# The last term of each block of attention scores, made in two halves of 144 columns

## The chip, the cores and the metric

One Trainium2 chip, one core. The metric is the device time of one execution in microseconds (us). Besides TensorE (PE in the profile; its weight loads are shown apart as PEld) the kernel uses VectorE (DVE), ScalarE (ACT), GpSimd (POOL) and SyncE's DMA queue (SP).

## The reference, cut to what matters

The program is an attention layer with a computed position bias (8 batches, 8 heads, 576 positions, 64 dimensions to a head), followed by a mixture of experts over the 4608 tokens. The change lies in `scores` alone, before the bias is added:

```python
scores = scale * np.matmul(q, k.transpose(0, 1, 3, 2))      # 576 x 576 for each batch and head
scores = scores + bias.transpose(2, 0, 1)[None, :, :, :]
scores = scores - np.max(scores, axis=-1, keepdims=True)
attn = np.exp(scores)
attn = attn / (np.sum(attn, axis=-1, keepdims=True) + 1e-09)
out = np.matmul(attn, v)
# then: softmax gate, the best of 8 experts for each token, relu(x @ w1[e]) @ w2[e], times the gate
```

## The kernel before, in words

The heads are taken two at a time: 32 pairs. The two heads of a pair lie one above the other on the partitions (64 dimensions each), so that a product of head 0 uses rows 0 to 63 of TensorE's array and the same product of head 1 rows 64 to 127. Of each pair the 576 queries make five blocks `c`. Blocks 0 to 3 hold 128 queries of each head; block 4 holds the last 64 queries of both heads, laid out as a block-diagonal tile, and so uses all 128 rows in one product. That makes 32 x 5 = 160 blocks of scores.

`scores` (the matmul is L372) makes one block in the PSUM tiles `sps`, one for each head, two banks each: the 576 keys are two `half`s of HS = 288 columns, one to a bank. `q` and `k` were split before into a high part, rounded to float32r, and the rest (`QK[:, 0]` and `QK[:, 1]`, both float32r, by `high` L338 on ACT and `low` L343 on DVE), and a product is a sum of three terms (`TERMS`): high x high, high x low, low x high, in this order, accumulated in PSUM. A block of two heads has 2 halves x 3 terms x 2 heads = 12 matmuls, head 0 and head 1 in turn; block 4 has 6. Every matmul loads its own weights, 128 query columns (64 or 128 rows).

`biased` (L395, DVE, one for each head) then reads a head's 576 scores from PSUM, adds the bias from `NBm` (block 4: `NBr`) and takes the row's extreme in the same instruction; `exps` (L409, ACT) makes the exponentials and their sums. `etrans` (through `turn`, L324) transposes the exponentials on TensorE, `av` (L488) multiplies them with `v`, in plain float32. There is one pair of `sps` tiles: the next block's first matmul of a head waits for that head's L395.

The order of the work is written out by hand in `ORDER`: five strings to a pair of heads, one step after the other for all engines (S is `scores`, E `exps`, T and t `etrans` and its evacuation, A and a `av`, and so on), pipelined over three pairs. Nothing looks at times; an engine takes its instructions in this order and waits on semaphores.

Behind the attention come the expert tiles: `phase1` (L1336), `phase2` (L1353), then pairs of tiles (L1427, L1439), all in float32r with the same three terms; their weights are read by SP's queue into `NBm`'s space (L1268, L1271) as it comes free.

Of the kernel before, what the change touches and what calls it, by code (L numbers as in the profile page):

```python
# [21 lines left out]
P = 128  # L22
# [6 lines left out]
HS = S // 2  # L29
QW = 512 + P  # L30
# [87 lines left out]
class Attn:  # L118
# [243 lines left out]
    def scores(self, n, c):  # L362

        nc = self.nc
        QK = self.QK[n % 2]
        qs = slice(P * c, P * c + P)
        for half in range(2):
            ks = slice(QW + HS * half, QW + HS * half + HS)
            for i, (a, b) in enumerate(self.TERMS):
                for h in range(2) if c < 4 else (None,):  # L370
                    o = slice(0, P) if h is None else slice(64 * h, 64 * h + 64)
                    nc.tensor.matmul(  # L372
                        self.sps[h or 0][:, half, 0:HS],
                        QK[o, a, qs],
                        QK[o, b, ks],
                        start=i == 0,
                        stop=i == 2,
                        tile_position=(0 if h is None else 64 * h, 0),
                        skip_group_check=True,
                    )  # L380
        self.E[n, c] = self.Eb[:, next(self.e_next)]
        return [self.biased(n, c, h) for h in range(2 if c < 4 else 1)]

# [1457 lines left out]
```

## Time and profile before

| what | value |
|---|---|
| median of 3 runs | 966.83 us (965.53 to 967.01) |
| profiled execution, time and span | 971.9 us, 970.1 us |
| PE busy | 944.8 us (97%), 10430 matmuls |
| PEld busy | 784.2 us (81%), 10430 loads |
| DVE, ACT, POOL busy | 679.0, 632.2, 233.0 us |
| granted TensorE clock, mean | 0.990 |

The span runs from the first to the last instruction of the profiled execution; 1.8 us lie around it. Matmuls are pipelined, and a matmul's row has its whole passage through the array, so neighbours overlap: what a matmul costs in a stream is the distance from one start to the next, not its duration. A pair of matmuls of the two heads starts within some ns of each other, on different rows of the array.

### The profile page before, as it was taken

To read this page: it belongs to the slowest core of one execution; us is meant where nothing else is said; L and a number is where in the kernel's file an instruction comes from. 1 tells how busy PE (TensorE), PEld (TensorE's weight loads), DVE (VectorE), ACT (ScalarE), POOL (GpSimd) and SP (SyncE) were. 2 spreads that over 40 slices of the span, in tenths; PEclk is the share of its full clock that TensorE was granted. 3 is DMA by queue.
4 is the path that set the end of the run, shared out by engine and by line. 5 is a ranking of instruction groups with operands and counts; after the bars stand their busy time and mean duration, and the time that the engine had idled before them with its cause. 6 is when DMAs were issued, how large, how long until landed. Compare 5 with 4: busy or idle time off the path is not lost.

```text
span 970.1 us, 26355 instructions
## 1 busy us (share of the span) xinstructions
PE 944.8 (97%) x10430; PEld 784.2 (81%) x10430; DVE 679.0 (70%) x1528; ACT 632.2 (65%) x1396; POOL 233.0 (24%) x388
## 2 busy tenths in 40 slices
PE   7979999999999999999998999999999999999997
PEld 5448888888888888888887888897577888888885
DVE  7978889899999989999975668855224444353434
ACT  7988889899998999989874555555123423242323
POOL 0002001323142322314633345131104031212111
PEclk9999999999999999999998999999999999999998
DMA  5875312322232233223161112367835320201111
GB/s 148 241 228 150 121 55 91 109 77 90 87 126 84 70 106 102 85 68 125 39 231 52 44 55 85 129 229 267 298 130 175 120 77 11 76 33 55 44 45 47
DMA packets 50586, 106.89 MB, mean 110 GB/s; under 512 B 14033, under 2 KB 16849, under 8 KB 50452
## 3 DMA queue, kind: packets, MB, share of 16 engines
q1 hardware_dynamic: 42676, 84.00, 26.4%
q0 software_dynamic: 7680, 21.10, 6.6%
q8 instruction: 84, 1.38, 0.6%
q14 instruction: 50, 0.41, 0.1%
q10 hardware_dynamic: 96, 0.00, 0.0%
HBM read 118.86 MB, written 22.00 MB: 145 GB/s over the span
## 4 chain that ended last, share of the span: by engine, by line
PE 83%; DMA 6%; issue 5%; SPq 2%; ACT 1%; DVE 1%; POOL 1%; ACTq 0%; DVEq 0%; POOLq 0%
PE sps L372 15%; PE xps L488 9%; PE eps L488 8%; PE p L1427 6%; PE p L1336 5%; PE xps L1439 5%; PE eps L324 5%; PE p L1439 5%; PE xps L324 5%; PE pq L1427 4%; PE bps L201 4%; DMA NBm<-moe_w 4%; PE p L1353 2%; PE xps L1353 2%; PE xps L427 1%
## 5 line engine op out<-in xcount | busy, mean ns | idle before, releaser
L409 ACT ACTIVATE Eb<-Eb,mn 128x576 f32<-128x576 f32 x288 | 223.3, 785 | 10.0 <-DVE mn L395 9.2
L395 DVE CUSTOM_DVE_ANT_0 Eb<-sps,NBm 128x576 f32<-128x576 f32 x256 | 183.3, 753 | 15.7 <-ACT rT L329 5.8
L372 PE MATMUL sps<-QK 64*128 64x288 f32 (+1 forms) x1728 | 175.0, 309 | 3.7 <-DVE mn L395 3.5
L372 PEld LDWEIGHTS sps<-QK 64*128 64x128 f32 (+1 forms) x1728 | 139.2, 188 | 12.3 <-issue 6.6
L1366 POOL DMA_INDIRECT out<-mo,idt x22 | 22.9, 1041 | 254.9 <-ACT mo L1363 243.6
L1429 ACT ACTIVATE hh<-p 128x512 fp32r<-128x512 f32 x28 | 16.8, 599 | 97.6 <-PE p L1427 87.6
L1430 DVE SCALAR_TENSOR_TENSOR hl<-p,hh 128x512 fp32r<-128x512 f32 x28 | 19.4, 691 | 84.0 <-ACT hh L1429 81.9
L488 PE MATMUL xps<-eT,v 128*64 128x160 f32 (+1 forms) x960 | 75.3, 299 | 0.0
L1304 DVE TENSOR_TENSOR w2lo<-NBm,w2hi 128x1024 fp32r<-128x1024 f32 x49 | 60.1, 1226 | 15.8 <-ACT w2hi L1303 15.3
L488 PE MATMUL eps<-eT,v 128*64 128x144 f32 (+1 forms) x992 | 70.7, 283 | 0.0
L418 POOL COPY rem<-Eb 128x128 f32<-128x128 f32 x64 | 18.7, 293 | 206.8 <-ACT Eb L409 172.5
L488 PEld LDWEIGHTS xps<-eT,v 128*64 128x64 f32 x960 | 58.4, 136 | 9.8 <-issue 9.5
L343 DVE TENSOR_TENSOR QK<-qk,QK 128x640 fp32r<-128x640 f32 (+1 forms) x64 | 61.7, 965 | 0.0
L329 ACT COPY eT<-xps 128x512 f32<-128x512 f32 (+1 forms) x127 | 59.3, 501 | 2.3 <-PE eps L324 0.8
L488 PEld LDWEIGHTS eps<-eT,v 128*64 128x64 f32 x992 | 56.6, 138 | 3.1 <-issue 2.8
L1336 PE MATMUL p<-QK,w1hi 128*128 128x256 f32 x384 | 56.4, 291 | 2.0 <-ACT w1hi L1310 2.0
L409 ACT ACTIVATION_READ_ACCUMULATOR Eb<-Eb,mn 128x1 f32 x288 | 57.9, 201 | 0.0
L870 POOL TENSOR_TENSOR xrb<-xrb,rec 128x512 f32<-128x512 f32 (+1 forms) x34 | 35.4, 1042 | 91.1 <-DVE xrb L331 47.9
L1427 PE MATMUL p<-QK,w1hi 128*128 128x512 f32 x224 | 56.0, 392 | 0.4 <-DVE htq L1670 0.4
L1336 PEld LDWEIGHTS p<-QK,w1hi 128*128 128x128 f32 x384 | 51.8, 199 | 2.8 <-ACT w1hi L1310 2.1
L1303 ACT CAST w2hi<-NBm 128x1024 fp32r<-128x1024 f32 x49 | 51.2, 1044 | 3.5 <-DMA NBm<-moe_w 3.5
L1278 POOL DMA_INDIRECT NBr<-xg,idt x40 | 44.0, 1099 | 33.7 <-issue 9.9
(339 smaller groups left out, 2217.7 us busy)
## 6 DMA issues: line engine op xcount, KB each, us to landing
NBm<-moe_w SPq DMA_DIRECT2D x14, 2048.0 KB
NBm<-moe_w SPq DMA_DIRECT2D x28, 1024.0 KB
qk<-qk SPq DMA_DIRECT2D x32, 608.0 KB
NBm<-moe_w SPq DMA_DIRECT2D x32, 512.0 KB
v<-v SPq DMA_DIRECT2D x32, 320.0 KB
xg<-xrb SPq DMA_DIRECT2D x28, 258.0 KB
NBm<-eT SPq DMA_DIRECT2D x10, 288.0 KB
NBm<-eT SPq DMA_DIRECT2D x20, 144.0 KB
```

The source lines that it names most:

```text
L324: self.nc.tensor.transpose(ps[r][0:n, col : col + 64], x[o, :], self.idf[o, o])
L329: self.nc.scalar.copy(out, ps)
L343: self.nc.vector.tensor_tensor(QK[:, 1, sl], self.qk[n][:, sl], QK[:, 0, sl].bitcast(F32), op=ALU.subtract)
L372: nc.tensor.matmul(self.sps[h or 0][:, half, 0:HS], QK[o, a, qs], QK[o, b, ks], start=i == 0, stop=i == 2, tile_position=(0 if h is None e ...
L395: nc.vector.tensor_tensor_reduce(out=e.rearrange("p (t w) -> p t w", t=2), in0=ps, in1=nb.rearrange("p (t w) -> p t w", t=2), scale=self.S ...
L409: self.nc.scalar.activation(e, e, AF.Exp, bias=mn, scale=-1.0, accum_out=sm)
L488: nc.tensor.matmul(ps[o, :], v[:, 4 * D * h + D * k : 4 * D * h + D * k + D] if k < 4 else v[:, 512 + D * h : 512 + D * h + D], eT[:, h, k ...
L1303: self.nc.scalar.copy(h, w)
L1304: self.nc.vector.tensor_tensor(l, w, h.bitcast(F32), op=ALU.subtract)
L1336: nc.tensor.matmul(ps[:, a, :], w[:, c, fs], x[:, c, :], start=i == 0, stop=i == len(ops) - 1)
L1427: nc.tensor.matmul(ps, w[:, c, fs], x[:, c, :], start=j == 0, stop=j == len(ops) - 1, skip_group_check=True)
L1439: nc.tensor.matmul(self.acc[w], h[:, P * w : P * w + P], m[:, f, :], start=f == 0 and j == 0, stop=f == NFC - 1 and j == 2, skip_group_che ...
```

## The change

The third term of the second half of each block (low x high, into columns 288 to 575) is issued as two matmuls for each head, of 144 columns each, into the two parts of the same PSUM columns. The order is: columns 0 to 143 for head 0, then head 1, then columns 144 to 287 for head 0, then head 1. Weights, operands and sums are the same as before. Blocks 0 to 3 have 14 matmuls in place of 12, block 4 has 7 in place of 6; each has its own weight load.

```diff
-            ks = slice(QW + HS * half, QW + HS * half + HS)
+            k0 = QW + HS * half
             for i, (a, b) in enumerate(self.TERMS):
-                for h in range(2) if c < 4 else (None,):
-                    o = slice(0, P) if h is None else slice(64 * h, 64 * h + 64)
-                    nc.tensor.matmul(
-                        self.sps[h or 0][:, half, 0:HS],
-                        QK[o, a, qs],
-                        QK[o, b, ks],
...
+                for ks in halves if (half, i) == (1, 2) else whole:
+                    for h in range(2) if c < 4 else (None,):
+                        o = slice(0, P) if h is None else slice(64 * h, 64 * h + 64)
+                        nc.tensor.matmul(
+                            self.sps[h or 0][:, half, ks],
+                            QK[o, a, qs],
+                            QK[o, b, k0 + ks.start : k0 + ks.stop],
...
```

Here `whole = (slice(0, HS),)`, `mid = HS // 2` and `halves = slice(0, mid), slice(mid, HS)`.

## Rows read from the trace of the kernel before

**Rows 1.** The page: the span, busy time by engine, TensorE's granted clock in 40 slices.
```profile
span 970.1 us, 26355 instructions
...
PE 944.8 (97%) x10430; PEld 784.2 (81%) x10430; DVE 679.0 (70%) x1528; ACT 632.2 (65%) x1396; POOL 233.0 (24%) x388
...
PEclk9999999999999999999998999999999999999998
```

**Rows 2.** The chain of work that ended last, 398 to 414 us: start, length, what.
```profile
400.88 0.98 PE sps L372 x6
401.86 0.65 PE xps L324 x16
402.50 0.50 PE eps L324 x16
403.00 0.91 PE sps L372 x12
403.91 1.51 PE xps L488 x20
405.42 0.34 PE eps L324 x8
405.77 0.87 PE sps L372 x12
406.63 1.38 PE xps L488 x20
408.01 0.64 PE eps L324 x15
```

**Rows 3.** Busy time of the engines in the attention, 110 to 490 us.
```profile
core 0: us, PE busy (x) PEld busy (x) DVE busy (x) ACT busy (x) POOL busy (x), PEclk, DMA share, GB/s
110.00:490.00 380.00, 379.79 (x6386) 330.57 (x6383) 347.02 (x933) 343.27 (x914) 106.92 (x228) 1.00 0.28 91
```

**Rows 4.** All waits of PE, 74 to 500 us: us in total, times, longest.
```profile
PE sps L372 <- DVE mn L395: 0.2, 1, 0.2
```

**Rows 5.** All of L372: durations in ns, shortest, median and longest.
```profile
L372 PEld LDWEIGHTS sps<-QK x1728: 182/185/333, 55.1 to 499.4; 64*128 64x128 f32 x192
L372 PE MATMUL sps<-QK x1728: 286/291/606, 55.1 to 499.6; 64*128 64x288 f32 x192
```

**Rows 6.** Timeline of PE, one block of two heads: start, us, line, tiles, count.
```profile
402.86 1.06 PE L372 MATMUL sps<-QK 64*128 64x288 f32 x12
403.84 1.31 PE L488 MATMUL xps<-eT,v 128*64 128x160 f32 x16
404.98 0.44 PE L488 MATMUL xps<-rT,v 128*64 128x160 f32 x4
```

**Rows 7.** Durations in ns of the same block's loads and matmuls.
```profile
L372 PEld LDWEIGHTS sps<-QK x12: 183/184/187, 402.9 to 403.5; 64*128 64x128 f32 x12
L372 PE MATMUL sps<-QK x12: 288/290/396, 402.9 to 403.6; 64*128 64x288 f32 x12
```

**Rows 8.** Timeline of PE, one block 4 and what follows it.
```profile
400.81 1.05 PE L372 MATMUL sps<-QK 128*128 128x288 f32 x6
401.79 0.59 PE L324 MATMUL xps<-idf,Eb 64*128 64x64 f32 x12
```

**Rows 9.** The chain in the expert tiles: unbroken runs of 256 and of 512 columns.
```profile
619.74 11.53 PE p L1336 x96
...
808.88 5.44 PE pq L1427 x24
```

**Rows 10.** Matmuls by line and shape: count, busy us, mean ns.
```profile
L372 PE MATMUL sps<-QK 64*128 64x288 f32 x1536 | 141.1, 309 | 2.8 <-DVE mn L395 2.7
L1336 PE MATMUL p<-QK,w1hi 128*128 128x256 f32 x384 | 56.4, 291 | 2.0 <-ACT w1hi L1310 2.0
L1427 PE MATMUL p<-QK,w1hi 128*128 128x512 f32 x224 | 56.0, 392 | 0.4 <-DVE htq L1670 0.4
L488 PE MATMUL xps<-eT,v 128*64 128x144 f32 x480 | 36.0, 292 | 0.0
L372 PE MATMUL sps<-QK 128*128 128x288 f32 x192 | 33.9, 312 | 0.8 <-DVE mn L395 0.8
```

**Rows 11.** Weight loads by line and shape, as above.
```profile
L372 PEld LDWEIGHTS sps<-QK 64*128 64x128 f32 x1536 | 112.8, 188 | 5.9 <-DVE mn L395 4.4 <-issue 1.3
L1336 PEld LDWEIGHTS p<-QK,w1hi 128*128 128x128 f32 x384 | 51.8, 199 | 2.8 <-ACT w1hi L1310 2.1
L1427 PEld LDWEIGHTS p<-QK,w1hi 128*128 128x128 f32 x224 | 41.7, 188 | 11.7 <-issue 2.5 <-DVE htq L1670 0.7
L1318 PEld LDWEIGHTS p<-idf,NBr 128*128 128x128 f32 x80 | 9.4, 140 | 1.3
```

**Rows 12.** Timeline of PE: the last early block of scores that waits, and the next.
```profile
70.78 2.48 PE L372 MATMUL sps<-QK 64*128 64x288 f32 x12 [0.99 <-DVE mn L395]
74.50 0.58 PE L372 MATMUL sps<-QK 64*128 64x288 f32 x1
```

**Rows 13.** PE busy and granted clock around that stretch.
```profile
core 0: us, PE busy (x), PEclk, DMA share, GB/s
...
70.00:72.00 2.00, 1.15 (x5) 0.65 1.00 408
72.00:74.00 2.00, 2.00 (x32) 0.50 0.48 103
74.00:76.00 2.00, 2.00 (x28) 0.50 0.31 26
76.00:78.00 2.00, 2.00 (x25) 0.65 0.57 165
```

**Rows 14.** Timeline of SP's queue: the first expert weights.
```profile
483.76 0.42 SPq L1268 DMA_DIRECT2D NBm<-moe_w  x1
501.16 1.07 SPq L1271 DMA_DIRECT2D NBm<-moe_w  x2
```

More of the change, by code (lines that the diff above doesn't have):

```diff
@@ L366, in scores @@
         qs = slice(P * c, P * c + P)
+        whole, mid = (slice(0, HS),), HS // 2
+        halves = slice(0, mid), slice(mid, HS)
         for half in range(2):
-            ks = slice(QW + HS * half, QW + HS * half + HS)
+            k0 = QW + HS * half
             for i, (a, b) in enumerate(self.TERMS):
-                for h in range(2) if c < 4 else (None,):
-                    o = slice(0, P) if h is None else slice(64 * h, 64 * h + 64)
-                    nc.tensor.matmul(
-                        self.sps[h or 0][:, half, 0:HS],
-                        QK[o, a, qs],
-                        QK[o, b, ks],
[L376 to L380, printed above, removed]
+                for ks in halves if (half, i) == (1, 2) else whole:
[5 more added lines that the diff above has]
+                            QK[o, b, k0 + ks.start : k0 + ks.stop],
+                            start=i == 0,
+                            stop=i == 2,
+                            tile_position=(0 if h is None else 64 * h, 0),
+                            skip_group_check=True,
+                        )
         self.E[n, c] = self.Eb[:, next(self.e_next)]
```

## The prediction

> **What bounds the kernel now.** I read the page's engines first, then the chain of waits, then the attention's own engines, and last one block of scores at the scale of single matmuls. The page has PE at 97% of the span [rows 1], but a busy PE means little, since matmul rows overlap. The chain says more: in the attention it runs over PE alone, from one group of matmuls to the next, with no other engine between them [rows 2], and the same holds from 74.5 us to the end of the scores at 499.6 us. In 380 us of that stretch PE has 379.8 us busy, DVE 347.0 and ACT 343.3 [rows 3], and from 74 to 500 us PE waits for another engine just once, for 0.2 us [rows 4]. So TensorE's own issue is the limit, and a nanosecond added to its stream there is a nanosecond added to the time. The one loop beside it, from a block's scores through DVE's two L395 to the next block's scores, begins with the same matmuls, and a later end of them moves it by as much as it moves PE.
>
> **What one block costs.** The 12 matmuls of a block lie in 1.06 us [rows 6], the last takes 0.290, so the last pair starts 0.77 us after the first. The first pair's matmuls take 396 ns and the others 290 [rows 7]: 106 ns more. I read this as a weight load that nothing hides, since these start with their load. The other steps are (770 - 106) / 5 = 133 ns from pair to pair. Block 4 gives (1050 - 290 - 106) / 5 = 131 ns for its single matmuls [rows 8].
>
> What a step consists of, the expert tiles show, which use the same type: 11.53 us / 96 = 120 ns for 256 columns, 5.44 / 24 = 227 ns for 512 [rows 9]. The 107 ns between them are 256 columns at 0.417 ns, one column in a cycle of 2.4 GHz, the level that rows 3 have granted (1.00). So 288 columns stream in 120 ns, 144 in 60, and 11 to 13 ns of a step are fixed.
>
> The weight load is the second clock of a step. Two loads of float32r weights can't follow each other faster than one takes, 106 ns by the first pair. At 288 and 512 columns that is hidden: the load's row is 188 ns in both, and 199 at 256 columns [rows 11], where stream and load are about equal, as if it had begun to be held up. The load's row for plain float32 weights of the same 128 columns is 140 [rows 11], so this type's load is the longer one.
>
> **The change, part by part.** Removed: one step of 288 columns at the end of each block (two matmuls, or one in block 4). Added: two steps of 144. Nothing else moves: no DMA, no DVE or ACT instruction, no wait; L395 waits for the last matmul of its head as before.
>
> - The first half starts where the whole one started; its load runs under the 288 columns ahead of it. Cost nothing; the cover is those 120 ns against a load of 106, and without it this load would add up to 106 ns.
> - The second half needs its own load, although the weights are the same: the kernel issues as many loads as matmuls (10430 of each, [rows 1]), so none is dropped for being the same as the one before. That load can begin when the first half begins to stream, and the first half streams for 60 ns only. So the second half starts not 60 + 13 = 73 ns but 106 + 12 = 118 ns after the first. From both sides: 73 ns if the load is hidden after all, 120 ns by the nearest row, the 256-column step [rows 9]. I take 118, nearest to that row.
> - The second half then streams for 60 ns in place of 120. Behind the block the next group changes the array's tiling (64 or 128 rows, 64 or 128 columns) and starts about 0.21 us after the last scores' start: 403.84 against 402.86 + 0.77 [rows 6], 120 of it the stream and some 90 the change. The 90 stay, and 60 of the 120 go. Block 4's follower has the same distance, 401.79 against 400.81 + 1.05 - 0.29, 0.22 us [rows 8].
>
> Net for each block: 118 + 60 - 120 = +58 ns, from +13 (hidden load) to +60.
>
> Blocks on the path: 160 in all (1536 / 12 = 128 of two heads and 192 / 6 = 32 blocks 4, [rows 10]), the last at 499.6 us [rows 5]. The first seven start before 74.5 us, while PE waits for DVE [rows 12], behind transfers and partly at half clock [rows 13]; of these I count two. 155 x 58 ns = 9.0 us; from 2.0 (13 ns) to 9.3 (60 ns).
>
> What comes later gives none of it back: the experts' first weights are issued at 483.8 and 501.2 us [rows 14], when the bias table's space comes free as the attention ends, so the rest shifts as a whole. DVE and ACT get a longer period for the same work.
>
> One rule of the Trainium skill speaks against the large term: "TensorE: Matmul & The Clock Gate", section "Back-to-back issue gap", gives N / 2.4 + 2.5 ns for a warm matmul on its own, 62.5 ns for 144 columns. By it the estimate is +2.5 ns a block and +0.4 us in all. The rows above have 13 ns where it has 2.5, and the 106 ns of an unhidden load stand against it here; its section "LDWEIGHTS (loading the stationary operand)" in the same page gives columns / 1.2, an estimate of 107 ns for 128, which the trace's 106 agrees with.
>
> **The sum.** The profiled execution took 971.9 us (span 970.1), 5.1 above the runs' median; it gives 971.9 + 9.0 = 980.9. The extra is in the attention's own stream, where the runs don't differ by more than their 1.5 us, so I put it on the median: 966.83 + 9.0 = 975.8.
>
> **The rivals.**
>
> - *The load is hidden (not slower).* Place: between the two halves. If the second load could start under the 288-column matmul ahead, 73 ns or less separate the halves, and the price is 13 ns a block, or 2.5 with a smaller fixed part: 0.4 to 2.0 us, 967.2 to 968.8, within 0.2%. It decides as soon as a load takes under about 73 ns of a step. For it: loads of a pair do run beside the other row half. Against: the 106 ns of a block's first pair, and the 256-column load's longer row. Chance 0.11.
> - *The narrow matmul loses its single pass.* No float32r matmul of this kernel is narrower than 256 columns, so its rate at 144 isn't shown. The plain float32 ones show what such a loss costs: `av` has 10 calls and 20 matmuls [rows 2, 6], each at (404.98 + 0.44 - 403.84 - 0.30 - 0.05) / 9 = 137 ns a pair for 160 columns (0.05 for its first load, half as wide as the scores'); the 144-column group is 0.13 us shorter [rows 2], 13 ns a pair: so two instructions to a product, and two cycles to a column, 123 ns at 144. With both, a block has four steps where one was: 3 x 123 = +369 ns, 57 us, 1024. With two cycles to a column alone, a half costs 120 + 13 and the end streams 120: +133 ns, 20.6 us, 987.4. For it: nothing but that the case is new; against: the rate is the same 0.417 ns from 256 to 512, and 288 lies on the line. Chances 0.14 and 0.10.
> - *Faster.* The half-clock stretch [rows 13] has about 6.8 us at 1.2 GHz and costs some 3.4 us. More matmuls in the blocks just ahead of it could end or move it; with the hidden load that would be 966.83 + 0.4 - 3.4 = 963.8. Against: PE there waits for transfers, which this change doesn't touch. Chance 0.03.
> - *Part of it is absorbed*, in waits of PE that the profile puts down to no one, which come with each change of tiling: +20 to +45 ns a block, 970 to 974. Chance 0.07.
>
> **How the numbers follow.** The forecast has 0.55: 975.8, its own range 974.5 to 977.0 (53 to 63 ns a block on 150 to 160 blocks, and the median's own spread). Beside it stand 0.11 hidden, 0.07 partly absorbed, 0.10 at 987.4, 0.14 at 1024 and 0.03 faster. A range from 967.8 to 988.5 holds the forecast, the absorbed case, the two cycles and most of the hidden case, 0.82; it leaves out the double pass and the faster case. A measurement here can tell about 0.2% (1.9 us) from no change. Slower by more: 0.55 + 0.07 + 0.10 + 0.14 and a little of the hidden case, 0.87; within 0.2%: 0.10; faster: 0.03.
>
> **What would show it.** In the profile after, a block's last weight load starts with the first half and the second half starts some 118 ns behind it; the matmul rows of 144 columns are about 60 ns shorter than the 290 of 288; the next group starts about 0.15 us after the last scores' start; the run from 110 to the attention's end is longer by 58 ns a block and PE waits as little as before. Wrong: halves 73 ns or 133 ns apart, more than 14 (7) matmul records in a block, or 144-column rows of 290 ns and more. If the halves are 118 ns apart and the time grows by much less than 9 us, then my claim that PE's stream alone sets the end is what fails.

## The result and the profile after

| | median, us | lowest to highest |
|---|---|---|
| before | 967.01 (5 runs) | 965.53 to 968.6 |
| after | 975.71 (5 runs) | 973.46 to 976.55 |

The changed kernel takes 1.0088 times as long, with a 95% interval of 1.0071 to 1.0105: 8.7 us more. The forecast was 975.8.

The page after, against [rows 1]:

```profile
span 973.8 us, 26931 instructions
...
PE 949.1 (97%) x10718; PEld 803.7 (83%) x10718; DVE 678.7 (70%) x1528; ACT 631.3 (65%) x1396; POOL 232.0 (24%) x388
...
PEclk9999999999999999999999999999999999999999
```

There are 288 more matmuls and as many more weight loads (10718 of each): 2 x 128 + 32, one for each matmul that became two. The other engines do what they did.

The matmuls and loads of the scores by line and shape (count, busy us, mean ns; L375 after is L372 before), against [rows 10, 11]:

```profile
L375 PE MATMUL sps<-QK 64*128 64x288 f32 x1280 | 122.8, 312 | 2.2 <-DVE mn L398 2.1
L375 PE MATMUL sps<-QK 64*128 64x144 f32 x512 | 47.5, 250 | 0.0
L375 PE MATMUL sps<-QK 128*128 128x144 f32 x64 | 10.9, 252 | 0.0
...
L375 PEld LDWEIGHTS sps<-QK 64*128 64x128 f32 x1792 | 128.6, 186 | 5.0 <-DVE mn L398 3.4 <-issue 1.3
```

The load's row is as long as before (186 against 188 ns), also before a half. The mean of 250 ns for 144 columns hides two kinds, which one block shows. PE's timeline of the block that answers to [rows 6] (start, length in us); the line below the dots is the same view of a window that only the block's last pair reaches into:

```profile
406.18 1.11 PE L375 MATMUL sps<-QK 64*128 64x288 f32 x14
407.22 0.36 PE L491 MATMUL xps<-eT,v 128*64 128x160 f32 x2
...
407.01 0.27 PE L375 MATMUL sps<-QK 64*128 64x144 f32 x2
```

The durations in ns (shortest, median, longest) of this block's matmuls, against [rows 7], and of its last pair alone:

```profile
L375 PE MATMUL sps<-QK x14: 227/291/398, 406.2 to 407.0; 64*128 64x288 f32 x10, 64*128 64x144 f32 x4
...
L375 PE MATMUL sps<-QK x2: 270/270/270, 407.0 to 407.0; 64*128 64x144 f32 x2
```

The first halves take 227 ns, 63 less than the 290 of 288 columns. The second halves take 270: 43 ns longer for the same columns. Their rows begin 66 ns behind the first halves' (starts in the trace, 768 and 834 ns after the block's), so they come to an end 66 + 43 = 109 ns behind them. I read a row that begins on time and lasts 43 ns too long as a matmul that waits inside its row for its weights; since the profile only models the ends of matmul rows, this needs a check by starts, which the run with half a load gives below. The last pair's loads start 770 ns after the block's first matmul, 2 ns behind the first half, as the forecast had it.

The block lasts 1.11 us where it lasted 1.06, and the next group starts 407.22 - 406.18 = 1.04 us after it where it was 0.98. Over the blocks 26 to 155 the median from a block's first start to the next group's is 1036.5 ns against 989, +47.5 ns, and in block 4 1037.5 against 992, +45.5.

The chain of waits in the attention is PE's alone, as in [rows 2] (start, length, what):

```profile
404.14 1.03 PE sps L375 x7
405.18 0.64 PE xps L324 x16
405.82 0.50 PE eps L324 x16
406.32 0.97 PE sps L375 x14
407.29 1.51 PE xps L491 x20
408.80 0.34 PE eps L324 x8
```

The steps beside the scores are as long as before; block 4 goes from 0.98 to 1.03, the block after it from 0.91 to 0.97. All waits of PE from 74 to 510 us, against [rows 4]:

```profile
PE sps L491 <- DVE mn L398: 0.6, 1, 0.6
PE eps L324 <- issue: 0.3, 1, 0.3
PE sps L375 <- DVE mn L398: 0.2, 1, 0.2
```

They are still next to nothing. In the same 380 us PE is busy for as long as before, and DVE and ACT have 5 to 6 us less to do, since less of the attention fits in (columns as in [rows 3]):

```profile
110.00:490.00 380.00, 379.79 (x6525) 342.54 (x6526) 341.45 (x917) 338.10 (x902) 106.18 (x228) 1.00 0.27 87
```

The two profiled executions differ by less than the medians, 975.7 against 971.9 us. They aren't alike in the clock: the one after has the half-clock stretch of [rows 13] for half as long (the granted clock is the third column from the right).

```profile
70.00:72.00 2.00, 1.61 (x12) 0.73 0.91 317
72.00:74.00 2.00, 2.00 (x39) 0.50 0.28 72
74.00:76.00 2.00, 2.00 (x34) 0.91 0.49 55
```

The second such stretch is shorter too and comes later: from 517 to 525 us the kernel before was granted 0.57, from 525 to 529 us the one after 0.58. So steps are compared below within the attention from block 25 on, where both have the full clock throughout.

### The profile page after: what moved, and what is told of

Its sections match the earlier page's. It is cut to its first block, busy times and chain, and to the rows that moved or that the text cites. A ratio compares the mean times of both kernels' runs of the same rounds, so it can differ in the third digit from the quotient of the medians.

```text
span 973.8 us, 26931 instructions
## 1 busy us (share of the span) xinstructions
PE 949.1 (97%) x10718; PEld 803.7 (83%) x10718; DVE 678.7 (70%) x1528; ACT 631.3 (65%) x1396; POOL 232.0 (24%) x388
## 4 chain that ended last, share of the span: by engine, by line
PE 87%; issue 5%; DMA 3%; DVE 1%; ACT 1%; POOL 1%; SPq 1%; POOLq 0%; DVEq 0%; ACTq 0%
PE sps L375 15%; PE xps L491 9%; PE eps L491 8%; PE p L1430 7%; PE p L1339 6%; PE xps L1442 5%; PE p L1442 5%; PE eps L324 5%; PE xps L324 5%; PE xps L1356 5%; PE pq L1430 4%; PE bps L201 4%; PE p L1356 2%; DMA NBm<-moe_w 2%; PE pq L1638 1%
## 5 line engine op out<-in xcount | busy, mean ns | idle before, releaser
L375 PE MATMUL sps<-QK 64*128 64x288 f32 (+3 forms) x2016 | 181.3, 294 | 3.0 <-DVE mn L398 3.0
L375 PEld LDWEIGHTS sps<-QK 64*128 64x128 f32 (+1 forms) x2016 | 159.3, 187 | 11.4 <-issue 6.6
```

Source lines behind the costliest of these rows:

```text
L375: nc.tensor.matmul(self.sps[h or 0][:, half, ks], QK[o, a, qs], QK[o, b, k0 + ks.start : k0 + ks.stop], start=i == 0, stop=i == 2, tile_po ...
```

## The experiments

The theory (A), made after the result: the second part of a split term waits for its own weight load, put at 107 ns (106 in [rows 7]), which begins when the first part begins to stream. With a cut at m columns a block then costs max(107, m / 2.4 + 13) + (288 - m) / 2.4 - 120 ns more. The rivals: a fixed price for each added matmul (B), and narrow matmuls that stream slower (C). Seven kernels were run on two chips (e1 to e4 on chip 7, e5 to e7 on chip 10), then the kernel before and two of the seven on a third (e8 to e10 on chip 3). The times are compared with runs of the kernel before on the same chip. "A block" is the median from a block's first start to the next group's, blocks of two heads, less the same in a trace of the kernel before: the one of the sections above for e1 to e4, whose chip isn't on record, and e8_before for the others. For e5 to e7 this compares two chips, on which the kernel before had the same median (961.54 and 961.58 us).

| run | median, us | before, us | ratio (95%) | A, ns a block | measured, ns a block |
|---|---|---|---|---|---|
| e1_cut256 | 969.72 | 967.29 | 1.0024 (1.0014 to 1.0034) | +13 | +6 |
| e2_cut32 | 983.18 | 967.29 | 1.0158 (1.0138 to 1.0177) | +94 | +97 |
| e3_middle_term | 983.32 | 967.29 | 1.0166 (1.0149 to 1.0183) | +81 | +86.5 |
| e4_quarters | 1006.09 | 967.29 | 1.0388 (1.0369 to 1.0408) | +231 | +231.5 |
| e5_narrow_load | 963.60 | 961.54 | 1.0020 (1.0011 to 1.0029) | +13 | +5.5 |
| e6_head_by_head | 970.56 | 961.54 | 1.0102 (1.0086 to 1.0117) | +154 or +47 | +50 |
| e7_after | 969.90 | 961.54 | 1.0093 (1.0078 to 1.0109) | +47 | +51 |
| e8_before | 961.39 | 961.58 | 1.0000 (0.9991 to 1.0010) | 0 | 0 |
| e9_narrow_again | 963.62 | 961.58 | 1.0019 (1.0010 to 1.0029) | +13 | +6 |
| e10_after_again | 970.80 | 961.58 | 1.0087 (1.0068 to 1.0106) | +47 | +49.5 |

**The cut at 256.**

```diff
-        whole, mid = (slice(0, HS),), HS // 2
+        whole, mid = (slice(0, HS),), 256
```

> The same edit with the cut at 256 of the 288 columns: 256, then 32. Theory A (the second part waits for its own weight load, 107 ns, which can only begin when the first part begins to stream): the load is hidden under the 107 ns of the 256 columns, so the step is an ordinary one, 107 + 13 = 120 ns, and the tail streams 13 ns: net 120 + 13 - 120 = +13 ns a block, x 155 = +2.0 us (ratio 1.002). Theory B (every added matmul has a fixed price, the +47 ns that the halves showed between a block's first start and the next group's): +47 ns, +7.3 us (1.0075). Theory C (matmuls under 256 columns stream slower, 0.535 ns a column, so that two halves cost +47): only the 32 columns are slow, 120 + 17 - 120 = +17 ns, +2.6 us.

PE's timeline of one block:

```profile
402.34 1.06 PE L375 MATMUL sps<-QK 64*128 64x288 f32 x14
```

The parts of the split term in this block by shape (count, busy us, mean ns):

```profile
L375 PE MATMUL sps<-QK 64*128 64x256 f32 x2 | 0.3, 278 | 0.0
L375 PE MATMUL sps<-QK 64*128 64x32 f32 x2 | 0.2, 175 | 0.0
```

As many matmuls and loads were added as by the change, and a block is no longer than before (1.06 us). B falls with this run. The price isn't in the number of instructions but in how wide the first part is. A has 13 ns and the trace 6: the second part starts 119 ns behind the first, as A has it, but the next group follows 112 ns behind that start where 224 - 107 = 117 were expected (medians; 224 is the kernel before's).

**The cut at 32.**

```diff
-        whole, mid = (slice(0, HS),), HS // 2
+        whole, mid = (slice(0, HS),), 32
```

> The same edit with the cut at 32: 32 columns, then 256. A: the 32 columns stream in 13 ns and hide next to nothing, the second part starts 107 ns behind the first and streams 107: net 107 + 107 - 120 = +94 ns a block, +14.6 us (1.015). B: +47 ns, +7.3 us. C: 32 x 0.535 + 13 + 107 - 120 = +17 ns, +2.6 us.

The timeline of the same block here:

```profile
412.31 1.16 PE L375 MATMUL sps<-QK 64*128 64x288 f32 x14
```

And the parts by shape:

```profile
L375 PE MATMUL sps<-QK 64*128 64x256 f32 x2 | 0.4, 361 | 0.0
...
L375 PE MATMUL sps<-QK 64*128 64x32 f32 x2 | 0.2, 174 | 0.0
```

The same two shapes in the other order cost 0.10 us a block. The 32-column row is as long as with the cut at 256 (174 and 175 ns), the 256-column row behind it 361 against 278: the 83 ns are the wait for the load. C falls, since it gives the same for both cuts.

**The middle term.**

```diff
-                for ks in halves if (half, i) == (1, 2) else whole:
+                for ks in halves if (half, i) == (1, 1) else whole:
```

> The halves of 144 in the second half's middle term in place of its last, so that a whole third term follows. A: nothing is given back at the end, and the third term's load is not hidden under 60 ns either: two steps of 107 in place of one of 133, net +81 ns a block, +12.6 us (1.013). B: +47 ns, +7.3 us. C: 2 x (144 x 0.535 + 13) - 133 = +47 ns, +7.3 us.

The timeline of the same block:

```profile
410.67 1.14 PE L375 MATMUL sps<-QK 64*128 64x288 f32 x14
```

+0.08 us against 1.06 in the block, as A has it: in the middle of a block two loads stand uncovered, and no shorter tail gives 60 ns back. The change costs only 47 because it sits at the end.

**Quarters.**

```diff
-        halves = slice(0, mid), slice(mid, HS)
+        halves = [slice(72 * k, 72 * k + 72) for k in range(4)]
```

> The last term in four parts of 72 columns: three matmuls (and loads) more where the halves have one. A: three steps of 107 and a tail of 30: 321 + 30 - 120 = +231 ns a block, +35.8 us (1.037). B: three times 47 = +141 ns, +21.9 us (1.023). C: 3 x (72 x 0.535 + 13) + 39 - 120 = +73 ns, +11.3 us (1.012).

The timeline of the same block:

```profile
431.64 1.30 PE L375 MATMUL sps<-QK 64*128 64x288 f32 x18
```

Its quarters by shape:

```profile
L375 PE MATMUL sps<-QK 64*128 64x72 f32 x8 | 0.5, 254 | 0.0
```

The block is 0.24 us longer than in [rows 6]. In the trace the rows of the four quarters end 110 to 112 ns behind each other (medians), a load each, where the stream of 72 columns takes 30 ns; their mean of 254 ns is longer than the 227 of the first halves with twice the columns. The weight loads themselves show the pace: in this block those of the third and fourth quarter start 108 and 112 ns behind the one before.

**Half a load.** The same matmuls and columns, with 64 weight columns in place of 128 for the second half; the third term is left out there for the other 64 queries.

```diff
+                        nq = 64 if ks.start == mid else P
...
-                            self.sps[h or 0][:, half, ks],
-                            QK[o, a, qs],
+                            self.sps[h or 0][0:nq, half, ks],
+                            QK[o, a, P * c : P * c + nq],
```

> As the changed kernel, but the second half of 144 columns loads only 64 of the 128 weight columns: it leaves out the third term of the other 64 queries in these 144 key columns. Same number of matmuls, same columns streamed, half the load. A: the load is 53 ns and hides under 60, the step is 60 + 13 = 73: net 73 + 60 - 120 = +13 ns a block, +2.0 us (1.002). B and C: nothing about the load matters, +47 ns, +7.3 us (1.0075), as the changed kernel.

The timeline of the same block:

```profile
401.49 1.07 PE L376 MATMUL sps<-QK 64*128 64x288 f32 x14
```

Its halves by shape:

```profile
L376 PE MATMUL sps<-QK 64*128 64x144 f32 x2 | 0.2, 227 | 0.0
L376 PE MATMUL sps<-QK 64*64 64x144 f32 x2 | 0.2, 226 | 0.0
```

The scores' weight loads of the whole run by shape, blocks of two heads:

```profile
L376 PEld LDWEIGHTS sps<-QK 64*128 64x128 f32 x1536 | 111.0, 186 | 5.5 <-DVE mn L399 4.0 <-issue 1.3
...
L376 PEld LDWEIGHTS sps<-QK 64*64 64x64 f32 x256 | 20.9, 131 | 0.0
```

The load's row goes from 186 to 131 ns, 55 less, and with it the 43 ns of waiting in the second half's row are gone: 226 against 270. The starts say the same: the next group follows the second half's start in 208 ns in the changed kernel and in 164.5 here (medians), 43.5 less. Otherwise this kernel differs from the changed one only by the results for the 64 queries that it leaves out. Together with the costs of e1 to e4, which A gives within 7 ns, that shows the load as the cause. Where the load is hidden A is 7 ns too high: the second half starts 66 ns behind the first here, not 73, so that the fixed part of this step is 6 ns and not 13.

**Head by head.**

```diff
-                for ks in halves if (half, i) == (1, 2) else whole:
-                    for h in range(2) if c < 4 else (None,):
+                for h in range(2) if c < 4 else (None,):
+                    for ks in halves if (half, i) == (1, 2) else whole:
```

> The halves of the last term in another order: both halves of head 0, then both of head 1. A, with matmuls started strictly in order: head 0's second half waits 107 for its load, head 1's first half can't start before it, and head 1's second half waits 107 more: 107 + 107 + 60 - 120 = +154 ns in the blocks of two heads, +47 in block 4: 124 x 154 + 31 x 47 = +20.6 us (1.021). A, with the two row halves free of each other: +47 ns, +7.3 us, as the changed kernel. B: +47 ns, +7.3 us (the same matmuls). C: the same, +7.3 us.

The timeline of the same block:

```profile
407.21 1.10 PE L377 MATMUL sps<-QK 64*128 64x288 f32 x14
```

The block is as long as in the changed kernel (1.10 and 1.11 us), not 0.1 us longer. So head 1's first half, which stands behind head 0's second half in PE's program, doesn't wait for it: the rows of the two first halves start 3 ns apart in the trace (760 and 763 ns after the block's), and the second halves 62 ns later. A row doesn't name its head, but only a head's second half signals a semaphore, which tells the halves apart: here the last two of the four rows do. So it is in 117 of e6's 128 blocks of two heads; in the other 11 one head's two halves start ahead of the other's. In the changed kernel, whose source has the heads in turn, the counts are 114 and 14.

**The changed kernel and the narrow load again, and a trace of the kernel before.**

> The changed kernel once more, beside the two above: +47 ns a block between a block's first start and the next group's, +7.3 us on 155 blocks; the runs so far had a median of +8.7 us. If these runs come to 7 and not to 9, the chain of blocks accounts for all of it.

> The kernel before itself, for a trace from the same chip as the two below and as a measure of what two sets of runs of one program differ by: ratio 1.000. If the burst sums are all there is, the stretch from the 25th to the 160th block of scores is as long as in the narrow-load kernel within 0.7 us (135 blocks x 4 to 5 ns), and shorter than the changed kernel's by 6.4 us (135 x 47.5).

> The narrow second load (it leaves out the third term of 64 queries in 144 key columns) once more: by its bursts +4 to +5 ns a block, 0.7 us in all (1.0007). If the earlier +2 us returns, some 1.3 us come from elsewhere, and its trace against that of the kernel before says in which stretch: the attention's, the start's or the experts'.

> The changed kernel once more on this chip: by its bursts +47.5 ns x 155 = +7.4 us (1.0076); by the runs so far +8.4 to +8.8 us (1.009). The same stretches are compared as for the narrow load.

These are kernels told of above, unchanged. From block 25 to block 160 the kernel before takes 376.90 us (e8), the narrow load 377.50 and 377.59 (e5, e9), the changed kernel 382.97 and 382.92 (e7, e10). That is +0.6 to +0.7 and +6.0 to +6.1 us for 135 blocks: 4 to 5 and 45 ns a block. The mean of the changed kernel is below its median because six blocks, 39, 59 and on to 139, which small matmuls (L827 before) follow, became shorter: their followers start 1068 to 1090 ns behind the block's start where it was 1109 to 1151 (first pair of traces). What they waited for is not shown. The span and the first and last matmul of the scores, of e8_before:

```profile
core 0 of [0], span 959.0 us
...
L372 PE MATMUL sps<-QK x1728: 285/292/403, 54.7 to 496.4; 64*128 64x288 f32 x192
```

And of e7_after, from the other chip:

```profile
core 0 of [0], span 967.2 us
...
L375 PE MATMUL sps<-QK x2016: 223/291/402, 54.7 to 503.3; 64*128 64x288 f32 x116, 64*128 64x144 f32 x47, 128*128 128x288 f32 x15, 128*128 128x144 f32 x6
```

Both start their scores at 54.7 us, neither has a half-clock stretch in the attention, and the last scores come at 496.4 and 503.3: +6.9 us. The spans differ by 8.2, so 1.3 us were added behind the attention. In e10_after_again, on e8's chip, what follows the last scores is 1.7 us longer (its attention had lost some 4 us before, in a stretch at half clock from 65 to 79 us). Matched matmul by matmul, the expert part runs level until PE waits for a transfer of expert weights some 180 us in, and the difference arises there. The chain of waits has that transfer, in e8_before (start, length):

```profile
671.83 9.85 DMA NBm<-moe_w
```

and in e7_after, 1.1 us longer:

```profile
678.92 10.91 DMA NBm<-moe_w
```

The length of this transfer doesn't go with the change in every pair of traces: in e10 it is 10.89 us, but in the first pair it took 11.06 before the change and 9.90 after it, and there the part behind the last scores became 1.5 us shorter.

## Why the prediction was right

- **PE alone sets the end in the attention: right.** +47.5 ns in a block's median became +45 ns a block from block 25 to 160.
- **The weights are loaded again for the second half and the load isn't hidden: right,** and shown by five runs: the price follows the width of the first part (e1, e2), two uncovered loads cost two (e3), three cost three (e4), and half the load costs nothing to speak of (e5). "TensorE: Matmul & The Clock Gate" of the Trainium skill, section "LDWEIGHTS (loading the stationary operand)", has columns / 1.2, an estimate of 107 ns for 128 columns; the waits here come to 106 to 112.
- **The step of 118 ns: mis-sized.** I added the fixed 12 ns of a streaming step to the load. The second halves end 109 ns behind the first. A step that waits for its load has next to no fixed part on top; 109 + 60 - 120 = +49 against the 47.5 measured. The sum would have been 155 x 47.5 = 7.4 us and not 9.0, and 47.5 lies outside the 53 to 63 ns of the forecast's own range.
- **How it would show: half wrong.** I expected the second half to start 118 ns behind the first and named 73 as a sign of being wrong. Its row starts 66 ns behind and is 43 ns longer. Whoever read the starts alone would have taken the load for hidden.
- **The tail gives 60 ns back: right.** The next group starts 407.22 - 407.01 = 0.21 us behind the last row's start, not 0.15, but 43 ns of these are the wait inside that row. e3, without a tail to shorten, costs 39 ns more than the change.
- **What comes later shifts as a whole: not quite.** The runs have +8.4 to +9.2 us (after, e7, e10), of which the blocks explain 7 to 8. The rest, 1.3 us in e7, stands at a transfer of expert weights; in the first pair of traces that part is shorter, so there the rest isn't located. The forecast's nearness to the measured time is in part luck, two errors that cancel: 1.6 us too much for the blocks, and 8.7 - 7.4 = 1.3 us that the blocks don't explain.
- **The profiled execution.** My 980.9 for a profile after was 5 us off. I had put the extra of the profile of before into the attention's own stream; what the traces show is a mean grant of 0.990 before and 0.996 after, and of the two longer half-clock stretches one, at 517 to 525 us, lies behind the attention. The median was the right base.

The rivals: the hidden load, at 13 ns a block, fell with the measured 47.5 and the 270 ns rows. With it fell what the Trainium skill, "TensorE: Matmul & The Clock Gate", section "Back-to-back issue gap", gives for a matmul on its own (an estimate of 62.5 ns for 144 columns), as the price of this change: +0.4 us; no run bears it out for a matmul whose load takes longer than its stream. Partial absorption, at 20 to 45 ns, comes nearest by size, but the groups beside the scores are as long as before, and what is missing from the 58 ns lies in the step itself, 109 for 118; only the six blocks named above absorb something. The loss of the single pass fell with the counts (10718 matmuls, one to a product), the two cycles to a column with the block's 47 ns, where they would have cost 133, and slower streaming of any size with e1 and e2. The rival that was faster, by way of the clock, wasn't seen: all five runs after lie above all five before.

What stays open: every variant is 0.5 to 2.9 us slower than its blocks explain, also e1, e5 and e9, in which a block costs 6 ns (in e1 block 25 to 160 is 1.5 us longer, 11 ns a block, since single blocks start late). In the traces of e5, e6, e7, e9 and e10 (chips 10 and 3) the part behind the last scores is 0.2 to 1.7 us longer than in e8_before, and the difference arises at the wait for expert weights; against the first trace of before, the traces of after and e1 to e4 are not longer there. Whether it belongs to the added instructions, to when the transfers start, or to chance was not settled.

None of the variants beats the kernel before: the best of the cuts tried, 256 + 32, costs nearly nothing in its blocks.

## What to carry to other kernels

In this kernel a matmul step cost the longer of its stream and the next weight load. Here 128 columns of float32r weights took 106 to 112 ns, and matmuls behind streams of 32, 72 and 144 columns were bound by their loads; an estimate from 107 ns for 256 columns [rows 9] puts the border at about 256. A split of one stream over the same weights pays for a second load. Where a split can't be avoided, put the wide part first and the narrow one last before a change of tiling: cut 256 + 32 cost 6 ns a block, 32 + 256 cost 97. Look at the row's length as well as at its start, and check a run whose sum comes out right step by step: here two errors of more than 1 us had cancelled.

## What the runs showed of the hardware that was not expected

- In e6 the two halves of the array's rows ran free of each other, mostly against the order of the source: in the block shown, a matmul on rows 64 to 127 started 3 ns after one on rows 0 to 63, and not behind the matmul that stands between them and waits for its weights. "TensorE: Matmul & The Clock Gate" of the Trainium skill, section "The mechanism", has matmuls strictly in the program's order, in start and end; for the starts on two row halves these traces differ: one program starts them in both orders (117 and 11 blocks in e6, 114 and 14 in the changed kernel).
- In block 4, which uses all 128 rows, the steps are 131 to 133 ns at 288 columns, not 106 + 120: a load is hidden under a matmul on the same rows. The same section of the Trainium skill has one sentence that lets a load overlap a running matmul only on other rows and one that also has a background weight buffer; this trace agrees with the second.
- A matmul that waits for its weights is shown as a long row, not as a gap: 270 against 227 ns for 144 columns, 361 against 278 for 256.
- The kernel before took 967.3 us on chip 7 and 961.5 and 961.6 on chips 10 and 3; why wasn't looked into.
